# One level of Strassen's algorithm in the first MoE layer of an attention and MoE kernel, with shared tile slots and a new order

## The chip, the core and the metric

The kernel runs on one NeuronCore of a Trainium2 chip. Its time is the device time of one execution in microseconds (us); a figure quoted for a kernel is the median over its runs. One core has a matrix engine (PE, whose weight loads the profile shows apart as PEld), a vector engine (DVE), an activation engine (ACT), a general engine (POOL), and a queue that issues data transfers (SP) to 16 DMA engines. Matmul results land in PSUM, eight banks of 2 KB per partition; everything else lives in SBUF.

## The reference

Local and global attention over 8 batches of 8 heads, then a two-layer MoE block over all 8 x 544 = 4352 rows:

```python
# attention: window of 32 to each side plus 32 global tokens; 512 local tokens, head_dim 64
k_all = concat([k_g, k_l]); v_all = concat([v_g, v_l])
out_g = softmax(scale * q_g @ k_all.T) @ v_all
s_ll = where(abs(i - j) <= 32, scale * q_l @ k_l.T, -1e9)
out_l = softmax(concat([scale * q_l @ k_g.T, s_ll])) @ concat([v_g, v_l])
x = concat([out_g, out_l]).transpose(0, 2, 1, 3).reshape(4352, 512)
# MoE: d_model 512, d_ff 2048
h = x @ w_in
g = where(h >= 1, h, where(h <= -1, 0, (h + 1) ** 2 / 4))
out = g @ w_out
```

## The kernel before

All products run in fp16 on PE. Each operand is held as a high and a low fp16 half (`j` = 0, 1), so one product of two operands is three matmuls: high x high, low x high, high x low.

**Steps.** The program is written as named steps. Those of a batch `b` (0 to 7): loads `Lk`, `Lq`, `Lv`; scales `sk`, `sq`, `sv`; `pk`, `pq`, `pv` split k, q, v into halves and turn them with a DMA transpose; `aa{b}{i}{pr}` (att_a) scores and softmax of two heads for the 128 queries of block i; `ab` (att_b) the product with v; `ax{b}{i}` (att_x) scales the result, splits it (an ACT cast, a DVE or POOL subtraction) and turns it with a DMA transpose of 256 KB; `ga`, `gb` the global queries. The weights come once: `wd`, `ws`, `wh` decode, scale and split w_in (16 blocks `w0` to `w15` of 128 hidden columns, in groups of four), `od`, `oh` do it for w_out.

**MoE.** A *tile* `s` (0 to 15) is 256 local tokens, half a batch (two blocks of att_x). A *group tile* `g0`, `g1` collects the 128 global tokens of four batches. For each pair of hidden blocks moe1 makes `h` in one PSUM bank with 2 x 12 matmuls (4 slices of d_model x 3 halves), 256 token columns wide in a tile and 128 in a group tile; each matmul is preceded by the load of its 128x128 weights. A tile has 8 such pieces, 192 matmuls. Then five instructions make `g`: ACT Relu, two DVE operations, an ACT cast to the high half, a POOL subtraction for the low half (in tiles 0 and 1 sometimes on DVE). moe2 multiplies `g` by w_out: per tile 2 x 48 matmuls 512 columns wide in a second kind of bank, then DVE scales them and a DMA stores them.

**Order.** Nothing in the program runs in the order in which it is written. `segments` cuts the steps into pieces by engine, with the buffers each needs; `schedule` lays them out with a table of costs, taking at every moment the piece with the least due time (`deadlines`) that can start and finds free buffers; `LATER` shifts due times of single steps, in us. What comes out is a fixed order for each of the engines and the SP queue, and each engine works through its own strictly. PSUM has 3 banks for `h` (ps_h, also used by turns and weight splits), 2 for moe2 and norms (ps_o), 2 for scores (ps_s), 1 for att_b (ps_x). SBUF tiles of each kind have slots of their own.

Of the kernel before, what the change touches and what calls it, by code (L numbers as in the profile page):

```python
# [43 lines left out]
class Sketch:  # L44


    def __init__(self):
        self.nc = bacc.Bacc("TRN2", target_bir_lowering=False, num_devices=1)
        self.tiles, self.sizes = {}, {}

    def tile(self, pool, shape, dtype, tag, bufs):
        key = f"{pool.name}.{tag}"
        t = self.nc.dram_tensor(f"sketch{len(self.tiles)}", shape, dtype, kind="Internal").ap()
        self.tiles[t.tensor.name] = (key, bufs, pool.space)
        n = mybir.dt.size(dtype)
        for d in shape[1:]:
            n *= d
        self.sizes[key] = max(self.sizes.get(key, 0), (n + 3) // 4 * 4)
        return t


class Memory:
# [6 lines left out]
    def tile(self, pool, shape, dtype, tag, bufs):  # L69
        key, slot = f"{pool.name}.{tag}", self.taken[f"sketch{self.n}"]  # L70
# [4 lines left out]
        if (key, slot) not in self.slots:  # L75
            nm = f"{pool.name}_{tag}_{slot}"
            self.slots[key, slot] = self.pools[pool.space].tile([128, self.sizes[key] // 4], F32 if pool.space else I32, tag=nm, name=nm)
        n = 1
# [146 lines left out]
def schedule(segs, tiles, hop, slack, landing, ahead):  # L225

    users, queue, slots, many, taken = {}, {}, {}, {}, {}
    for g in segs:
        for nm in g.uses:
            users[nm] = users.get(nm, 0) + 1  # L230
        for nm in g.new:
            tag, n, _ = tiles[nm]
            queue.setdefault(tag, []).append(nm)
            slots[tag] = list(range(n))
            many[tag] = n
        g.left, g.ready = len(g.after), 0.0
    head = {tag: 0 for tag in queue}
    place = {nm: i for q in queue.values() for i, nm in enumerate(q)}
    engines = ("tensor", "vector", "scalar", "gpsimd", "sync")
# [6 lines left out]
    while len(order) < len(segs) or events:  # L246
        went = True
        while went:
            went = False
            for e in engines:  # L250
# [3 lines left out]
                for at, (_, _, g) in enumerate(waiting[e]):  # L254
                    if g.ready > now:
                        continue
                    need = {}
# [15 lines left out]
                for nm in sorted(g.uses - taken.keys(), key=place.get):  # L273
                    tag = tiles[nm][0]
                    taken[nm] = slots[tag].pop(0)
# [18 lines left out]
        if not events:  # L294
            done_ = {g.n for _, g in order}
            g = next((g for g in segs if g.n not in done_), None)
            if g:
                where = [(nm, tiles[nm], place[nm], head[tiles[nm][0]], slots[tiles[nm][0]], [m for m in queue[tiles[nm][0]] if users[m] and place[m] < head[tiles[nm][0]]], queue[tiles[nm][0]][head[tiles[nm][0]]]) for nm in g.new]
# [3 lines left out]
        while events and events[0][0] <= now:  # L302
# [11 lines left out]
            for nm in g.uses:  # L314
                users[nm] -= 1
                if users[nm] == 0:
                    slots[tiles[nm][0]].append(taken[nm])
# [30 lines left out]
def attention_moe(nc, memory, q_l, k_l, v_l, q_g, k_g, v_g, w_in, w_out, out):  # L348
# [19 lines left out]
    class Pool:  # L368
        def __init__(self, name, bufs, space=None):
            self.name, self.bufs, self.space = name, bufs, space  # L370
# [4 lines left out]
    pool = Pool  # L375
# [3 lines left out]
    gp = pool("hidden", 1)  # L379
    stg = pool("stage", 4)  # L380
    tmp = pool("tmp", 4)
    natp = pool("nat", 2)
    ktp = pool("kt", 7)
    kt4p = pool("kt4", 2)
    qtp = pool("qt", 3)
    qgp = pool("qg", 2)
    vp = pool("v", 7)
    v2p = pool("v2", 2)
    sm = pool("small", 2)
    bsm = pool("batch_small", 2)  # L390
    tp = pool("tts", 3)
    pfp = pool("pf", 2)
    ptp = pool("pt", 3)
    pgp = pool("pg", 1)
    xtp = pool("xt", 2)
    xgp = pool("xg", 1)
    xnp = pool("xn", 1)
    rp = pool("moe_t", 2)
    jp = pool("junk", 1)
    ps_h = pool("ps_h", 3, space=PSUM)  # L400
    ps_o = pool("ps_o", 2, space=PSUM)
    ps_s = pool("ps_s", 2, space=PSUM)
    ps_x = pool("ps_x", 1, space=PSUM)
# [59 lines left out]
    def all_sum(o, x, name):  # L463
# [3 lines left out]
        t = ps_s.tile([P, 1], F32, tag="s", name=f"as{name}")  # L467
# [3 lines left out]
    def all_max(o, x, name):  # L471
# [3 lines left out]
        t = ps_s.tile([P, P], F32, tag="s", name=f"am{name}")  # L475
# [19 lines left out]

    W = {}
# [6 lines left out]
    wi = [t.bitcast(F16).rearrange("p (j k c) -> p j k c", j=2, c=P) for t in wi32]  # L503
    wo = [t.bitcast(F16).rearrange("p (j c) -> p j c", j=2) for t in wo32]
# [38 lines left out]
    def w_scale(norms, tag, n, pl):  # L543
# [4 lines left out]
        inverse(t2, s, e, 2.0 ** -51, 2.0 ** -13)  # L548
# [17 lines left out]
    def halves(w, a, s, sid, who):  # L566
# [3 lines left out]
        if who[0] == "e":  # L570
            o = ps_h.tile([P, DM], F32, tag="h", name="wps")
# [22 lines left out]
    def turn(who, o, i):  # L594
# [5 lines left out]
        t = ps_h.tile([P, 8, P], F16, tag="h", name="turn")  # L600
# [765 lines left out]
```

## Time and profile before

| | us |
|---|---|
| runs: median (lowest to highest) of 3 | 972.21 (970.84 to 973.53) |
| profiled execution: first to last instruction | 972.9 |
| PE busy in it | 894.0 |
| DVE busy | 696.5 |
| ACT busy | 582.3 |
| POOL busy | 374.9 |

The profiled execution has no time of its own beside its span; the span stands 0.7 us above the median of the runs, inside their spread. Busy times are unions of the instructions' spans, so two that overlap count once. Matmuls are pipelined: the mean time of one matmul in a group is its way through the array, and what it costs the engine is the distance from one to the next, which the rows that merge a run of matmuls give (their us divided by their count).

### The profile page before, as it was taken

What the parts mean: (1) busy time and instruction counts of PE and PEld (TensorE: products, weight loads), DVE (VectorE), ACT (ScalarE), POOL (GpSimd) and SP (SyncE); (2) the same over time, 40 slices, a digit from 0 to 9 for tenths busy, and PEclk for the clock granted to TensorE, in tenths of its full rate; (3) what the DMA queues carried; (4) which work ended last, traced back from release to release, by engine and by line L of the source; (5) the groups of instructions that cost most, each with busy time, mean ns of one, the idle gap of its engine ahead of it and who ended that gap; (6) DMA issues with size and microseconds to landing.
All of it is one profiled execution on the core that took longest, in us unless ns stands there. A gap on an engine that the chain in (4) does not pass through costs nothing.

```text
span 972.9 us, 24493 instructions
## 1 busy us (share of the span) xinstructions
PE 894.0 (92%) x9375; PEld 633.7 (65%) x9375; DVE 696.5 (72%) x1951; ACT 582.3 (60%) x1405; POOL 374.9 (39%) x390
## 2 busy tenths in 40 slices
PE   0864879987999999999999999999999999999998
PEld 0443657556766776767676777767776777676764
DVE  3889898777876797678754977778767886564432
ACT  4898677666765666567553666567655754344221
POOL 9055655433324333332432424433433343332121
PEclk9877889997999999999999999999999999999999
DMA  9959669699896879789961888678877755244001
GB/s 254 241 138 216 161 135 161 152 161 164 136 187 131 148 135 168 125 139 152 168 128 24 136 148 177 115 131 153 138 153 136 138 113 109 56 86 51 23 2 33
DMA packets 386998, 129.41 MB, mean 133 GB/s; under 512 B 363328, under 2 KB 372544, under 8 KB 386880
## 3 DMA queue, kind: packets, MB, share of 16 engines
q1 hardware_dynamic: 386880, 127.85, 69.1%
q8 instruction: 73, 1.20, 0.5%
q14 instruction: 45, 0.37, 0.1%
HBM read 43.52 MB, written 8.91 MB: 54 GB/s over the span
## 4 chain that ended last, share of the span: by engine, by line
PE 67%; DMA 11%; DVE 8%; ACT 6%; issue 4%; POOL 2%; SPq 1%; ACTq 0%; DVEq 0%; POOLq 0%
PE ps_h_h L1280 30%; PE ps_o_o L1280 28%; PE ps_s_s L1280 5%; PE ps_x_x L1280 4%; DMA pt_pt<-const_pb 3%; DMA stage_st<-in_k_l_dram 2%; DMA qt_qa<-nat_nat 1%; ACT junk_junk L1280 1%; DMA stage_st<-in_moe_w_out_dram 1%; ACT pf_pf L1280 1%; DVE tts_t L1280 1%; DMA stage_st<-in_v_l_dram 1%; POOL const_pb L1280 1%; DVE tmp_tmp L1280 1%; DVE weights_w L1280 1%
## 5 line engine op out<-in xcount | busy, mean ns | idle before, releaser
L1280 PE MATMUL ps_h_h<-xt_xt,weights_w 128*128 128x256 f16 (+1 forms) x3456 | 383.5, 269 | 1.9 <-DVE moe_t_r L1280 1.4
L1280 PE MATMUL ps_o_o<-weights_w,hidden_g 128*128 128x512 f16 x1632 | 374.0, 380 | 3.0 <-DVE tmp_tmp L1280 1.1
L1280 PEld LDWEIGHTS <-weights_w 128*128 128x128 f16 x3456 | 320.8, 99 | 52.3 <-issue 5.0
L1280 POOL TENSOR_TENSOR hidden_g<-moe_t_r,hidden_g 128x512 f16<-128x512 f32 (+1 forms) x142 | 164.4, 1158 | 314.9 <-ACT hidden_g L1280 304.8
L1280 PEld LDWEIGHTS <-hidden_g 128*128 128x128 f16 x1712 | 158.7, 98 | 183.2 <-issue 17.0
L1280 POOL TENSOR_TENSOR const_pb<-pf_pf,const_pb 128x384 f16<-128x384 f32 (+1 forms) x117 | 120.6, 1032 | 225.7 <-DVE const_pb L1280 89.4
L1280 DVE SCALAR_TENSOR_TENSOR ps_h_h<-ps_h_h,batch_small_ms,moe_t_r 128x512 f32<-128x512 f32 (+1 forms) x144 | 104.2, 724 | 105.5 <-ACT moe_t_r L1280 105.3
L1280 ACT ACTIVATE pf_pf<-tts_t,small_nb 128x192 f32<-128x192 f32 (+1 forms) x256 | 117.0, 458 | 97.2 <-DVE small_nb L1280 77.3
L1280 ACT ACTIVATE moe_t_r<-ps_h_h,batch_small_ms 128x512 f32<-128x512 f32 (+1 forms) x144 | 107.8, 749 | 103.9 <-PE ps_h_h L1280 92.4
L1280 ACT CAST hidden_g<-moe_t_r 128x512 f16<-128x512 f32 (+1 forms) x144 | 84.4, 587 | 76.5 <-DVE moe_t_r L1280 76.2
L1280 DVE CUSTOM_DVE_ANT_0 tts_t<-ps_s_s,const_mask,batch_small_q 128x192 f32<-128x192 f32 (+1 forms) x256 | 98.9, 427 | 23.0 <-PE ps_s_s L1280 22.7
L1280 DVE SCALAR_TENSOR_TENSOR moe_t_r<-moe_t_r,batch_small_ms,ps_h_h 128x512 f32<-128x512 f32 (+1 forms) x144 | 102.5, 713 | 2.6
L1280 ACT ACTIVATE junk_junk<-stage_st 128x512 f16<-128x512 f32 (+1 forms) x108 | 67.5, 625 | 45.5 <-DMA stage_st<-in_k_l_dram 14.1
L1280 PE MATMUL ps_x_x<-v_v,pt_pt 128*128 128x64 f16 (+1 forms) x1536 | 68.8, 195 | 10.2 <-DMA pt_pt<-const_pb 7.7
L1280 DVE CAST const_pb<-pf_pf 128x384 f16<-128x384 f32 (+1 forms) x109 | 47.8, 440 | 41.0 <-ACT pf_pf L1280 23.0
L1280 PE MATMUL ps_s_s<-kt_kt,qt_qa 128*128 128x128 f16 (+2 forms) x704 | 69.3, 200 | 8.3 <-DVE small_nb L1280 5.7
L1280 PEld LDWEIGHTS <-pt_pt 128*128 128x128 f16 (+1 forms) x1536 | 61.8, 99 | 22.9 <-DMA pt_pt<-const_pb 10.9
L1280 PEld LDWEIGHTS <-qt_qb 128*128 128x128 f16 x704 | 55.4, 99 | 16.0 <-issue 10.8
L1280 PE MATMUL ps_s_s<-kt_kt,qt_qb 128*128 128x128 f16 (+2 forms) x704 | 65.8, 199 | 0.0
L1280 PEld LDWEIGHTS <-qt_qa 128*128 128x128 f16 x704 | 59.6, 99 | 6.3 <-issue 1.1
L1280 ACT ACTIVATION_READ_ACCUMULATOR pf_pf<-tts_t,small_nb 128x1 f32 x256 | 47.7, 187 | 0.0
L1280 PE MATMUL ps_o_o<-tmp_tmp,const_ones 128*128 128x128 bf16 (+1 forms) x76 | 14.3, 311 | 23.5 <-DVE tmp_tmp L1280 23.4
(170 smaller groups left out, 914.3 us busy)
## 6 DMA issues: line engine op xcount, KB each, us to landing
weights_w<-in_moe_w_in_dram SPq DMA_DIRECT2D x32, 256.0 KB, 4.1
stage_st<-in_q_l_dram SPq DMA_DIRECT2D x32, 256.0 KB, 4.2
qt_qb<-qt_qa SPq DMA_DIRECT2D x64, 128.0 KB, 2.7
stage_st<-in_moe_w_out_dram SPq DMA_DIRECT2D x32, 256.0 KB, 3.7
out_dram<-tmp_tmp SPq DMA_DIRECT2D x30, 256.0 KB, 2.6
stage_st<-in_k_l_dram SPq DMA_DIRECT2D x24, 256.0 KB, 3.8
stage_st<-in_v_l_dram SPq DMA_DIRECT2D x21, 256.0 KB, 4.4
v_v<-v_v SPq DMA_DIRECT2D x16, 128.0 KB, 3.2
```

Of the source, the lines that this page charges most:

```text
L1280: getattr(getattr(tc.nc, engine), op)(*a, **k)
```

## The change

**Strassen.** From tile 3 on (`T["fast"] = 3`), and for both group tiles, the product of w_in and the tokens is cut into 2 x 2 blocks: two groups of four hidden blocks (`f1`, `f2`), two halves of d_model, two halves of the tokens (128 + 128 in a tile, 64 + 64 in a group tile). Seven products P1 to P7 take the place of eight; each is 4 x 6 = 24 matmuls, 128 (or 64) columns wide. A tile has two such rounds (`q` = 0, 1), 2 x 7 x 24 = 336 matmuls. The sums around them: three sums of w_in blocks per round are made once, by matmuls with the identity (`combine`, steps `cb`) into six 4 KB tiles, and one difference overwrites its block of w_in when tile 2 is done with it (`replace`, steps `rp`). The sums of tokens are made per tile in att_x by four POOL subtractions of 256 columns, so that a tile now has four casts, four low halves and four DMA transposes where it had two of each (widths 512, 256, 512, 512 in place of 512, 512). The sums of products are formed in PSUM (P6, P7, P4 add to the bank of P1, P3 to that of P5), with three ACT copies and three DVE additions per round. `g` is made as before, for 4 hidden blocks x 128 tokens at a time, eight times per tile.

**Widths.** Tiles 0 to 2 make `h` for 128 tokens at a time instead of 256: 384 matmuls of 128 columns. The scale of w_in is now common to two groups, so their splits (`wh`) wait for both.

**Rooms.** SBUF tiles of up to 2 KB per partition share 48 slots, all PSUM tiles share the 8 banks, with a cap per kind (`ps_h` 4, `ps_o` 3, `ps_s` 2, `ps_x` 1). `LATER` is a new table that covers the steps of all batches.

```diff
@@ schedule
-                    if need and any(len(slots[tag]) < len(x) + (min(x) > head[tag]) or max(x) - head[tag] >= many[tag] for tag, x in need.items()):
+                    if need and (any(many[tag] - live[tag] < len(x) + (min(x) > head[tag]) or max(x) - head[tag] >= many[tag] for tag, x in need.items())
+                                 or any(len(slots[key]) < len(x) + (min(x) > first[key]) * (ROOMS[key][2] if key in ROOMS else 0) for key, x in rooms.items())):
...
@@ att_x
+        if t == 0 or not FAST(s):
+            XT[s, t] = across(xf, f"x{s}_{t}", who, how)
+            d["xn"] = xf
+            return
+        x1, x2 = d.pop("xn"), xf
+        XT[s, "b"] = across(x2[:, K:], f"xb{s}")
+        for o, y, z in ((x1[:, :K], x2[:, :K], x1[:, :K]), (x2[:, :K], x2[:, K:], x2[:, :K]), (x2[:, K:], x2[:, K:], x1[:, :K]), (x1[:, K:], x1[:, K:], x2[:, K:])):
+            nc.gpsimd.tensor_tensor(out=o, in0=y, in1=z, op=ALU.subtract)
+        XT[s, "c"] = across(x1, f"xc{s}")
+        XT[s, "d"] = across(x2, f"xd{s}")
...
+    def combine(q, a):
...
+        add(ident, f2, 0, True)
+        add(ident, f2, 1)
+        for n, (f, c) in enumerate((((0, 0), (f1, 0), (f1, 1)))):
+            if n:
+                add(negid, f, c)
+            o, sign = CW[q][n][:, a:a + 2], (1.0, 1.0, -1.0)[n]
+            nc.scalar.activation(o[:, :, 0], ps, AF.Copy, scale=sign)
+            nc.vector.scalar_tensor_tensor(o[:, :, 1], ps, sign, o[:, :, 0], op0=ALU.mult, op1=ALU.subtract)
...
+    def moe_f(key, d, x, n, q):
...
+        one = acc("x")
+        prod(one, "P1", True)
+        s = fold(who, "s", n)
+        nc.scalar.copy(s, one)
+        two = acc("z")
+        prod(two, "P5", True)
+        p5 = fold(who, "p", n)
+        nc.scalar.copy(p5, two)
+        prod(one, "P6", False)
+        u2 = fold(who, "u", n)
+        nc.scalar.copy(u2, one)
+        three = acc("y")
+        prod(three, "P2", True)
+        nc.vector.tensor_tensor(out=three, in0=three, in1=s, op=ALU.add)
+        out_of(three, 0, 0)
+        prod(one, "P7", False)
+        nc.vector.tensor_tensor(out=p5, in0=one, in1=p5, op=ALU.add)
+        prod(two, "P3", False)
+        nc.vector.tensor_tensor(out=two, in0=two, in1=u2, op=ALU.add)
+        out_of(two, 0, 1)
+        out_of(p5, 1, 1)
+        prod(one, "P4", False)
+        out_of(one, 1, 0)
...
+CAPS = dict(hidden=8, stage=9, tails=3, tmp=4, ob=3, nat=4, kt=7, qa=3, qb=3, v=7, v2=2, t=5, pt=3, xt=8, xg=1, xn=2, xh=2, r=5, raw=4, sums=6,
+            ps_h=4, ps_o=3, ps_s=2, ps_x=1)
+ROOMS = dict(room=(2048, 48, 4), twin=(4096, 6, 0), bank=(2048, 8, 0))
...
-LATER = {"Lk01": -7.5, "Lk10": 41.8, "Lk11": -14.2, "Lk12": 16.3, "Lk20": 29.4, "Lk21": -32.6, "Lk22": 17.4, "Lo0": 11.5,
+LATER = {"Lk00": -99.8, "Lk01": 23.8, "Lk02": 37.7, "Lk10": 212.4, "Lk11": -53.4, "Lk12": 178.5, "Lk20": 42.4, "Lk21": 24.7,
...
```

PE at the start of tile 9, before (weights `w0` is the first hidden block, `xt` the turned tokens, `ps_h` the bank of `h`):

```order
L1280 MATMUL ps_s_s_0_106<-kt_kt_6_197,qt_qb_2_152 128x64
L1280 LDWEIGHTS weights_w0_0_66
L1280 MATMUL ps_h_h_2_111<-xt_xt_0_139,weights_w0_0_66 128x256
...
L1280 LDWEIGHTS weights_w1_0_67
L1280 MATMUL ps_h_h_2_111<-xt_xt_0_139,weights_w1_0_67 128x256
```

PE in the first round of tile 9, after: the end of P5 (the `twin` tiles are sums of w_in, the first `room` of a moe1 row the tokens), a piece of moe2, then P6 and P3:

```order
L1440 LDWEIGHTS twin_4_168
L1440 MATMUL bank_1_108<-room_44_121,twin_4_168 128x128
L1440 LDWEIGHTS room_45_135
L1440 MATMUL bank_5_145<-weights_w0_0_66,room_45_135 128x512
...
L1440 LDWEIGHTS twin_5_171
L1440 MATMUL bank_2_128<-room_18_133,twin_5_171 128x128
...
L1440 LDWEIGHTS twin_0_155
L1440 MATMUL bank_1_108<-room_29_109,twin_0_155 128x128
```

Each matmul is half as wide and still loads its own weights; between P5 into bank 1 and P3 into the same bank ACT has to copy it, and the order puts 12 matmuls of moe2 and the 24 of P6 there.

PE during the attention of batch 1, before: the end of tile 1's moe1 (`w15`), followed by att_b of block 0:

```order
L1280 LDWEIGHTS weights_w15_0_81
L1280 MATMUL ps_h_h_0_102<-xt_xt_1_142,weights_w15_0_81 128x256
L1280 LDWEIGHTS pt_pt_1_138
L1280 MATMUL ps_x_x_0_160<-v_v_6_206,pt_pt_1_138 128x64
```

The same place after: the scores of block 0, then the first sum of w_in blocks (`cb`, with the identity as weights), then att_b:

```order
L1440 LDWEIGHTS room_24_132
L1440 MATMUL bank_3_105<-room_9_86,room_24_132 128x64
L1440 LDWEIGHTS const_ident_0_85
L1440 MATMUL bank_5_145<-weights_w4_0_70,const_ident_0_85 128x256
...
L1440 MATMUL bank_5_145<-weights_w5_0_71,const_ident_0_85 128x256
L1440 LDWEIGHTS room_8_98
L1440 MATMUL bank_1_108<-room_6_164,room_8_98 128x64
```

Eight of the 64 matmuls of `cb` stand ahead of att_b here; the others follow in pieces of 4 and 8 between the pieces of batch 1's attention, and all of `rp` between the last pieces of tile 2 and the first of tile 3.

DVE in tile 9, before (a piece's first operation writes `ps_h`, its second `moe_t_r`; the cast belongs to attention):

```order
L1280 SCALAR_TENSOR_TENSOR ps_h_h_2_111<-ps_h_h_2_111,batch_small_ms_0_171,moe_t_r_0_173 128x512
L1280 SCALAR_TENSOR_TENSOR moe_t_r_1_172<-moe_t_r_1_172,batch_small_ms_0_171,ps_h_h_1_112 128x512
L1280 TENSOR_SCALAR small_nb_2_143<-small_nb_2_143 128x2
L1280 CAST const_pb0_0_61<-pf_pf_0_131 128x2x224
L1280 SCALAR_TENSOR_TENSOR ps_h_h_0_102<-ps_h_h_0_102,batch_small_ms_0_171,moe_t_r_1_172 128x512
```

DVE in tile 9, after: an addition of a product's bank and a copy stands ahead of an output's two operations, and the low halves of att_x come in between:

```order
L1440 TENSOR_TENSOR bank_3_105<-bank_3_105,room_40_134 128x512
L1440 SCALAR_TENSOR_TENSOR bank_2_128<-bank_2_128,batch_small_ms_0_177,room_28_194 128x512
L1440 SCALAR_TENSOR_TENSOR room_2_88<-room_2_88,batch_small_ms_0_177,room_24_132 128x512
L1440 SCALAR_TENSOR_TENSOR room_28_194<-room_28_194,batch_small_ms_0_177,bank_2_128 128x512
L1440 TENSOR_TENSOR bank_7_131<-bank_7_131,room_1_143 128x512
L1440 SCALAR_TENSOR_TENSOR bank_3_105<-bank_3_105,batch_small_ms_0_177,room_37_150 128x512
```

The two operations per output are the same as before; the additions are new rows in the same queue.

## Rows read from the trace of the kernel before

**Rows 1.** The page: busy time of engines; 40 slices in tenths.
```profile
span 972.9 us, 24493 instructions
PE 894.0 (92%) x9375; PEld 633.7 (65%) x9375; DVE 696.5 (72%) x1951; ACT 582.3 (60%) x1405; POOL 374.9 (39%) x390
PE   0864879987999999999999999999999999999998
PEclk9877889997999999999999999999999999999999
```

**Rows 2.** Stretches: length; busy PE, PEld, DVE, ACT, POOL (count); clock, DMA share, GB/s.
```profile
0.00:300.00 300.00, 229.09 (x2301) 158.68 (x2302) 237.52 (x672) 214.86 (x509) 141.83 (x158) 0.90 0.85 176
300.00:850.00 550.00, 546.81 (x5949) 393.31 (x5948) 405.76 (x1157) 327.34 (x814) 202.86 (x201) 1.00 0.72 131
850.00:973.00 123.00, 118.11 (x1128) 81.71 (x1125) 53.26 (x123) 40.08 (x83) 30.19 (x33) 0.99 0.21 39
```

**Rows 3.** Shorter stretches, the same columns: three of 20 us, one of 50 us.
```profile
200.00:220.00 20.00, 17.27 (x183) 10.88 (x181) 14.81 (x53) 11.74 (x37) 7.24 (x7) 0.92 0.99 154
220.00:240.00 20.00, 14.59 (x247) 12.10 (x246) 16.88 (x63) 12.20 (x38) 5.27 (x8) 0.74 0.99 165
260.00:280.00 20.00, 20.00 (x190) 12.89 (x188) 17.73 (x50) 15.44 (x36) 5.61 (x6) 1.00 0.99 158
...
750.00:800.00 50.00, 50.00 (x596) 36.42 (x594) 41.86 (x128) 30.25 (x75) 19.36 (x19) 1.00 0.70 137
```

**Rows 4.** PE's groups by shape: count, busy us, mean ns, idle before.
```profile
L1280 PE MATMUL ps_h_h<-xt_xt,weights_w 128*128 128x256 f16 x3072 | 360.3, 275 | 1.9 <-DVE moe_t_r L1280 1.4 <-DMA xt_xt<-xn_xh 0.5
L1280 PE MATMUL ps_h_h<-xt_xt,weights_w 128*128 128x128 f16 x384 | 23.2, 219 | 0.0
```

**Rows 5.** The chain that ended last, pieces: start us, us, what.
```profile
303.66 2.62 PE ps_h_h L1280 x24
306.28 0.35 PE ps_x_x L1280 x12
306.63 2.59 PE ps_o_o L1280 x12
```

**Rows 6.** Timeline in group tile g1: start, us, engine, what.
```profile
941.47 4.22 PEld L1280 LDWEIGHTS <-weights_w 128*128 128x128 f16 x72
941.68 4.18 PE L1280 MATMUL ps_h_h<-xt_xt,weights_w 128*128 128x128 f16 x72
...
945.70 2.75 PE L1280 MATMUL ps_o_o<-weights_w,hidden_g 128*128 128x512 f16 x12
```

**Rows 7.** What PE waited for, 300 to 850 us: total, times, longest.
```profile
PE ps_x_x L1280 <- ACT xg_xgf L1280: 1.6, 1, 1.6
PE ps_x_x L1280 <- DMA pt_pt<-const_pb: 1.2, 2, 0.7
```

**Rows 8.** DVE's, ACT's and POOL's groups by shape, as in rows 4.
```profile
L1280 DVE SCALAR_TENSOR_TENSOR ps_h_h<-ps_h_h,batch_small_ms,moe_t_r 128x512 f32<-128x512 f32 x128 | 96.4, 754 | 91.2 <-ACT moe_t_r L1280 91.0
L1280 DVE TENSOR_TENSOR xn_xn<-ps_x_x,small_rc 128x512 f32<-128x512 f32 x32 | 22.0, 686 | 13.5 <-PE ps_x_x L1280 13.5
L1280 DVE TENSOR_TENSOR xn_xh<-xn_xn,xn_xh 128x512 f16<-128x512 f32 x27 | 19.3, 715 | 5.0 <-ACT xn_xh L1280 4.9
L1280 ACT ACTIVATE moe_t_r<-ps_h_h,batch_small_ms 128x512 f32<-128x512 f32 x128 | 98.8, 773 | 88.9 <-PE ps_h_h L1280 80.1 <-POOL hidden_g L1280 6.0 <-PE ps_s_s L1280 2.1
L1280 ACT CAST weights_w<-ps_h_h 128x512 f16<-128x512 f32 x12 | 6.6, 570 | 0.0
L1280 POOL TENSOR_TENSOR hidden_g<-moe_t_r,hidden_g 128x256 f16<-128x256 f32 x16 | 11.7, 728 | 32.4 <-ACT hidden_g L1280 28.6 <-issue 3.3 <-POOL hidden_g L1280 0.5
```

**Rows 9.** DMA transposes of att_x: count, median us from issue to landing.
```profile
xt_xt<-xn_xh SPq DMA_TRANSPOSE x32, 3.3
```

**Rows 10.** Timeline of the end, as in rows 6.
```profile
962.76 5.34 PE L1280 MATMUL ps_o_o<-weights_w,hidden_g 128*128 128x512 f16 x24
...
968.92 1.76 SPq L1280 DMA_DIRECT2D out_dram<-tmp_tmp  x4
```

More of the change, by code (lines that the diff above doesn't have):

```diff
@@ L225, in schedule @@
 def schedule(segs, tiles, hop, slack, landing, ahead):
-    users, queue, slots, many, taken = {}, {}, {}, {}, {}
+    users, queue, slots, many, taken, live, line = {}, {}, {}, {}, {}, {}, {}
     for g in segs:
@@ L273, in schedule @@
                 for nm in sorted(g.uses - taken.keys(), key=place.get):
-                    tag = tiles[nm][0]
-                    taken[nm] = slots[tag].pop(0)
+                    tag, _, _, key = tiles[nm]
+                    taken[nm] = slots[key].pop(0)
+                    live[tag] += 1
+                    while first[key] < len(line[key]) and line[key][first[key]] in taken:
+                        first[key] += 1
                     while head[tag] < len(queue[tag]) and queue[tag][head[tag]] in taken:
@@ L297, in schedule @@
             if g:
[L298 removed]
+                where = [(nm, tiles[nm], place[nm], head[tiles[nm][0]], slots[tiles[nm][3]]) for nm in g.new]
                 raise AssertionError(f"stuck at {g.n} {g.engine} {g.calls[0][0]} {g.uses} needs {[p for p in g.after if p not in done_]} {where}")
@@ L908, in att_a @@
             if "pbx" not in d:
[L909 removed]
+                d["pbx"] = [gp.tile([P, 2, 2, 256], F16, tag="g", name=f"pbx{n}") for n in range(2)]
                 for x in d["pbx"]:
@@ L1041, in attention_moe, with fold, act, middle @@
     GT = {}
-    def moe1(key, d, xt, n, f):
-        h = ps_h.tile([P, 2, n], F32, tag="h", name=f"h{key}_{f}")
-        for u in range(2):
+    def fold(key, nm, n):
+        return rp.tile([P, WG, n], F32, tag="r", name=f"{nm}{key}")
+    def act(key, d, h, n, g, o, low="p"):
+        c = slice(g, g + 1)
+        r = fold(f"{key}_{g}", "r", n)
+        nc.scalar.activation(r, h, AF.Relu, bias=d["hs"][:, c], scale=d["a1"][:, c])
+        nc.vector.scalar_tensor_tensor(h, h, d["a2"][:, c], r, op0=ALU.mult, op1=ALU.max)
+        nc.vector.scalar_tensor_tensor(r, r, d["sg"][:, c], h, op0=ALU.min, op1=ALU.mult)
+        nc.scalar.copy(o[:, :, 0], r)
+        (nc.vector if low == "v" else nc.gpsimd).tensor_tensor(o[:, :, 1], r, o[:, :, 0], op=ALU.subtract)
+    def middle(key, g, t):
+        if (key, g, t) not in GT:
+            GT[key, g, t] = gp.tile([P, WG, 2, P], F16, tag="g", name=f"gt{key}_{g}_{t}")
+        return GT[key, g, t]
+    def moe1(key, d, x, g, t):
+        h = ps_h.tile([P, WG, P], F32, tag="p", name=f"h{key}_{g}_{t}")
+        for u in range(WG):
             m = 0
@@ new lines, in replace @@
+    def replace(q, a):
+        K = DM // 2
+        ps = ps_h.tile([P, 2, 2, P], F32, tag="p", name=f"wr{q}{a}")
+        f1, f2 = 2 * WG * q + a, 2 * WG * q + WG + a
+        n = 0
+        for u in range(2):
+            for i, f in ((ident, f1), (negid, f2)):
+                for j in range(2):
+                    nc.tensor.matmul(ps[:, u], i, w16[f + u][:, j, :K], start=n == 0, stop=True, skip_group_check=True)
+                    n += 1
+        for u in range(2):
+            nc.scalar.copy(wi[f2 + u][:, 0, 0:2], ps[:, u])
+            nc.vector.tensor_tensor(out=wi[f2 + u][:, 1, 0:2], in0=ps[:, u], in1=wi[f2 + u][:, 0, 0:2], op=ALU.subtract)
```

311 lines of the change are left out of this document (185 added, 126 removed), and 150 rows, old and new, of the table LATER.

## The prediction

> **What bounds the kernel now.** The page first [rows 1]: of a span of 972.9 us PE is busy 894.0, and its slices read 9 from the eleventh to the last but one, while of the first ten only two do. Then the stretches [rows 2]: from 300 to 850 us PE is busy 546.81 of 550 at a granted clock of 1.00, with DVE at 405.76 (74%), ACT at 327 and POOL at 203; after 850 us it stays full to the end. Before 300 us it is idle 70.9 us, and the clock averages 0.90. So there are two regimes: a front of 300 us that waits for loads, for the decoding of weights and for the first attention (DVE 237.5 of 300, DMA 0.85), and a stage of 670 us in which PE's own work is the time. In that stage PE's waits, as the trace names them, come to little over 3 us in all, of which two rows stand for the most [rows 7]. What is taken off PE after 300 us should shorten the span by as much, unless something else comes to wait; work added ahead of 300 us may hide in PE's gaps.
>
> **The change, part by part, on PE.** The chain gives what a matmul costs PE [rows 5]: 24 of 256 columns take 2.62 us, 109.2 ns each; 12 of 64 columns 0.35 us, 29.2 ns each; 12 of 512 columns 2.59 us, 216 ns each. At 128 columns the kernel has group tile g1: 72 matmuls, each with its own weight load, stand between 941.68 and 945.70 us, where the next group begins [rows 6]; 4.02 us, 55.8 ns each.
>
> - Fast tiles (3 to 15, thirteen): 192 x 109.2 = 20.97 us become 336 x 55.8 = 18.75 us. Less 2.22 us each, 28.8 us in all.
> - Group tiles: 192 x 55.8 = 10.71 us become 336 x 29.2 = 9.81 us. Less 0.9 us each, 1.8 us.
> - Tiles 0 to 2: 384 x 55.8 = 21.43 us for 20.97, 1.4 us more.
> - `cb`: 64 matmuls of 256 columns, 7.0 us. `rp`: 32 of them, 3.5 us.
>
> That is 30.6 us less and 11.9 us more, net 18.7 us less.
>
> What the additions cost on the path depends on where they stand. The order puts `cb` between the pieces of batch 1's attention. There PE is idle 2.7 and 5.4 us in two stretches of 20 us and the clock falls to 0.74 [rows 3], so at most all 7.0 us hide; but `cb` also brings 12 ACT copies and 12 DVE operations of 512 columns, about 9 us of DVE at 754 ns [rows 8], and DVE is busy 31.7 of those 40 us. I take half, 3.5 us, with 0 and 7 as bounds. `rp` and the narrower tiles meet a PE that is full (20.00 of 20 from 260 to 280 us [rows 3]); I take them whole, 4.9 us.
>
> **On the other engines.** Per fast tile DVE gains six additions of 512 columns from PSUM (686 ns, as the row that scales an attention block [rows 8]), 4.1 us, and one and a half low halves (715 ns), 1.1 us: 5.2 us. ACT gains six copies from PSUM, between 570 and 773 ns each (the cast out of `ps_h` and the Relu [rows 8]), 3.4 to 4.6 us, and 1 us of casts. POOL gains four subtractions of 256 columns at 728 ns, 2.9 us. SP issues two transposes more per tile. A transpose of att_x lands 3.3 us after its issue [rows 9], which bounds the DMA time of one and a half more by 5 us per tile; the lower bound is what 384 KB take at the 131 GB/s that the stage moves at a DMA share of 0.72, 3 us at most [rows 2].
>
> Does any of them become the bound? moe1 of the stage from 300 to 850 us covers some 10.5 tiles and a group tile. DVE would come to 405.8 + 10.5 x 5.2 = 460 of about 526 us, 88%; ACT to 73%, POOL to 44%, DMA to between 0.81 and 0.85. DVE's 88% is high, but busy here counts the way of an instruction through the pipeline, and from 750 to 800 us DVE is at 41.86 of 50 with PE at 50.00 [rows 3]. What counts is then the meeting points inside a round: P6 needs the bank of P1 copied, P7 that of P6, P3 that of P5, P4 the addition after P7. The order puts 24 or more other matmuls between each pair, 1.34 us at least, while a copy takes 0.6 to 0.8 us plus ACT's queue. I put 3 us for added waits in the stage; the lower bound is 0, the upper one is the rival below.
>
> **The front's order.** All loads, decodes and the attention of batches 0 and 1 are laid out anew, with freer slots. Up to tile 3 each engine does the same work as before plus `cb` and `rp`. The front's idle 70.9 us are what a better order could draw on and a worse one could add to; nothing in the trace prices an order. I take 3 us less, with 12 less and 10 more as bounds, about a sixth of the idle time.
>
> **Sum.** 972.9 - 30.6 + 3.5 + 4.9 + 3 - 3 = 950.7 us. The profiled span is 0.7 us above the runs' median, so 950 us. The end is no term: after the last matmuls (962.76 + 5.34 us) come one DVE scaling and a store [rows 10], and both stay.
>
> **A rule against this.** The row shows 55.8 ns for a matmul of 128 columns with its weight load, sustained over 72 of them, and the loads take 4.22 us for the 72 beside them [rows 6]. The Trainium skill, page "TensorE: Matmul & The Clock Gate", section "Back-to-back issue gap", gives for streams of weight loads and matmuls a sustained 81 ns at 128 columns and 131 ns at 512. By it 336 matmuls would take 27.2 us, 6.2 us more than a tile's moe1 takes now, and thirteen tiles would lose 81 us: the change would be a large loss. The trace does not agree at either width (55.8 ns at 128 and 216 ns at 512 [rows 5]), so the sum goes by the rows, and the rule stands below as a rival.
>
> **The rivals.**
>
> *The front gains more than 3 us.* The order covers all steps and `cb` fills gaps in which the clock had dropped. For it: the 70.9 idle us. Against it: DVE at 79% over the whole front [rows 2], and no less work for it. With 12 us from the front and `cb` hidden, 972.2 - 30.6 + 4.9 - 12 = 934.5; chance 0.12 of a time below 942.
>
> *Waits in the fast tiles take half of the gain.* DVE at 88% runs late in stretches with attention, and PE meets it four times a round. At 0.11 us for each of the 120 meeting points (13 tiles and 2 group tiles, 2 rounds, 4 each) 13 us are lost: 963. For it: DVE's share. Against: 84% without a wait now. Chance 0.16 of 960 to 969.
>
> *Slower: the bank that is copied too late.* In a fast round PE can't go on in the bank of P1 until ACT, strict in its order, has copied it. If ACT or DVE stands behind attention work at these points (one operation of 512 columns ahead in a queue is 0.6 to 0.8 us [rows 8]), each of the 120 points may cost 0.4 us, 48 us in all: 972.2 - 22 + 48 = 998. It decides from 0.2 us a point (22 us / 120). For it: three of eight banks are held through a round, where a piece now holds one. Against: the trace shows PE waiting for a freed `h` bank almost never (idle 1.9 us before 3072 matmuls [rows 4]). Chance 0.07, at 975 to 1000.
>
> *The weight load sets the pace at 128 columns.* If long runs of such matmuls went at what the loads of moe1 take when they don't overlap, the fast tiles would lose; already at 62.4 ns a matmul (20.97 us / 336) a fast tile takes as long as now. Group tile g1's 55.8 ns, and the 0.0 us of idle time ahead of its 384 [rows 4], speak against it. At 70 ns, 13 x 336 x 14.2 ns = 62 us more than summed: 1012. Chance 0.01. (The skill's rule above would give this case.)
>
> *The change does not pay.* The front loses 10 us, `cb` lies on the path whole and the stage waits 8 us: 950 + 13 + 3.5 + 5 = 971. Chance 0.05.
>
> **How the numbers follow.** The forecast, 942 to 960, has 0.59; with 0.12 below and 0.16 between 960 and 969. A change of 0.3% (2.9 us) is about what this measurement can tell from none, so all of these count as faster: 0.87. The 0.05 of no gain is within 0.3% for the most part, 0.04, and 0.01 goes to slower, with the 0.07 and 0.01 of the two rivals: 0.09. For the range I leave out 0.05 below 936 and about 0.14 above 967.
>
> **What would show it.** In the profile of the changed kernel, 24 matmuls of 128 columns in a tile's moe1 take 1.34 us; if 1.5 or more, the load paces them. PE's busy time falls by 15 to 20 us and its idle time in the first 300 us stays within 10 us of 71. From 300 to 850 us PE reads at least 99% busy; 97% would mean the second rival, and PE rows of a fast tile that wait for ACT or DVE the third. DVE rises to 85 to 90% in that stage. The prediction is wrong if the stage after 300 us is not 25 to 29 us shorter for the same work, or if the front moves by more than 12 us.

## The result and the profile after

The changed kernel takes 946.16 us (median of 4 runs, 945.80 to 948.33), the kernel before 971.6 beside it: a ratio of 0.9732, with a 95% interval from 0.9711 to 0.9752. The prediction of 950 us, within 936 to 967, holds. That is in part luck: what Strassen's level saves was put too high and the gain of the front too low, as the experiments show.

The page of the changed kernel, the lines that answer to [rows 1]:

```profile
span 944.0 us, 30674 instructions
PE 861.5 (91%) x12204; PEld 642.3 (68%) x12207; DVE 786.0 (83%) x2079; ACT 642.9 (68%) x1545; POOL 434.0 (46%) x450
PE   0466889998989998999999999999999999999998
PEclk9979999999999999999999999999999999999999
```

The span is 28.9 us shorter; PE's busy time falls by 32.5 us and its idle time rises by 3.6. By the ratio of the runs the gain is 26.0 us: the two profiled executions stand further apart than the medians. Every run that lists both has a time 1.7 to 2.1 us above its span (945.80 and 944.0 us here), so the 972.9 us of before belong to a time near 975 us, above all its runs and not close to their median; the 945.80 us are the shortest of the changed kernel's runs. The work that was counted off PE is only 18.7 us. The clock line tells where most of the rest is from: before, six of the first ten slices stand below 9, now one. Its three stretches, against [rows 2] with the same columns:

```profile
0.00:300.00 300.00, 229.64 (x3123) 173.72 (x3126) 248.62 (x694) 225.79 (x543) 144.33 (x159) 0.98 0.86 180
300.00:850.00 550.00, 541.59 (x7951) 407.04 (x7949) 484.56 (x1294) 379.83 (x937) 258.73 (x258) 1.00 0.80 141
850.00:944.00 94.00, 90.27 (x1138) 61.54 (x1135) 52.81 (x93) 37.33 (x68) 30.89 (x34) 1.00 0.17 37
```

In the first 300 us PE is busy as long as before (229.64 for 229.09) and so idle as long, 70.4 us, but at a clock of 0.98 instead of 0.90. From 300 to 850 us DVE is at 88%, as summed, and PE at 98.5%. Two of the shorter stretches of [rows 3], and one with the most work on DVE:

```profile
220.00:240.00 20.00, 18.20 (x359) 16.24 (x357) 18.89 (x60) 15.16 (x40) 9.54 (x12) 1.00 0.82 112
260.00:280.00 20.00, 16.77 (x187) 10.72 (x185) 15.79 (x44) 12.98 (x33) 7.12 (x8) 1.00 0.78 168
...
600.00:700.00 100.00, 99.67 (x1444) 75.05 (x1443) 95.83 (x263) 75.30 (x192) 48.31 (x45) 1.00 0.94 160
```

Where the clock stood at 0.74, from 220 to 240 us, it is 1.00; where PE was full, from 260 to 280 us, it now has gaps; and DVE reaches 96% from 600 to 700 us while PE is busy 99.67 of the 100. The seven products of a round cost what [rows 6] said. The timeline of PE inside a fast tile (start, us, what) has three of them in a row, 1.34 us from one start to the next, 55.8 ns a matmul (the 1.50 us of a line count the last matmul's way through the array as well):

```profile
610.34 1.50 PE L1440 MATMUL bank<-room,twin 128*128 128x128 f16 x24
611.68 1.50 PE L1440 MATMUL bank<-room,weights_w 128*128 128x128 f16 x24
613.02 1.50 PE L1440 MATMUL bank<-room,twin 128*128 128x128 f16 x24
```

PE's waits from 300 us on (total, times, longest), against [rows 7]:

```profile
PE bank L1440 <- DMA room<-const_pb: 4.3, 3, 2.1
PE bank L1440 <- ACT room L1440: 2.1, 1, 2.1
PE bank L1440 <- DMA room<-room: 1.1, 1, 1.1
PE bank L1440 <- DVE room L1440: 0.8, 2, 0.4
```

That is 8 us where there were 3. More than half is waiting for the turned probabilities of an attention block (`const_pb`, turned by a DMA transpose), in three places; the copies and additions inside the fast rounds, 120 meeting points, show at most three waits (the rows for ACT and DVE). The new instructions beside PE, against [rows 8]:

```profile
L1440 DVE TENSOR_TENSOR bank<-bank,room 128x512 f32<-128x512 f32 x52 | 35.6, 692 | 18.0 <-PE bank L1440 17.8 <-ACT room L1440 0.2
L1440 DVE SCALAR_TENSOR_TENSOR room<-room,batch_small_ms,bank 128x512 f32<-128x512 f32 x102 | 75.0, 739 | 0.5
L1440 DVE SCALAR_TENSOR_TENSOR room<-room,batch_small_ms,room 128x512 f32<-128x512 f32 x52 | 49.2, 947 | 0.6 <-ACT room L1440 0.2
L1440 ACT COPY room<-bank 128x512 f32<-128x512 f32 x78 | 44.2, 579 | 17.1 <-PE bank L1440 15.8 <-POOL small_amv L1440 0.5 <-ACT room L1440 0.5
L1440 POOL TENSOR_TENSOR room<-room,room 128x256 f32<-128x256 f32 x39 | 32.3, 827 | 5.6 <-DVE room L1440 2.8 <-DVE batch_small_ms L1440 0.5 <-DVE small_nb L1440 0.5
```

The addition and the copy cost what was taken for them, POOL's subtraction 827 ns where 728 were taken. DVE's operations that make `g` look dearer where the sum lies in SBUF, as it does for one output in four: 947 ns for 739. The mean misleads here. The same operations with shortest, median and longest time (both widths):

```profile
L1440 DVE SCALAR_TENSOR_TENSOR room<-room,batch_small_ms,bank x114: 461/739/749, 110.6 to 926.0; 128x512 f32<-128x512 f32 x102, 128x256 f32<-128x256 f32 x12
L1440 DVE SCALAR_TENSOR_TENSOR room<-room,batch_small_ms,room x60: 466/747/1740, 299.6 to 922.4; 128x512 f32<-128x512 f32 x52, 128x256 f32<-128x256 f32 x8
```

Of the 52 wide ones 36 take 744 ns on average. The other 16 take 905 to 1740 ns, and each of them ends between 542 and 551 ns after a POOL operation beside it has ended. One of them, and the POOL operation:

```profile
805.71 1.74 DVE L1440 SCALAR_TENSOR_TENSOR room<-room,batch_small_ms,room 128x512 f32<-128x512 f32 x1
805.74 1.16 POOL L1440 TENSOR_TENSOR room<-room,room 128x512 f16<-128x512 f32 x1 [2.03 <-ACT room L1440]
```

So what costs DVE time is not the place of the sum as such: these operations, with both tensors in SBUF, are held up by POOL in 16 of 52 cases. The operations that read one tensor from a bank and write to SBUF, 102 as wide, stay at 749 ns or less, and of those that read and write a bank one in 102 goes beyond 759.

### The profile page after: what moved, and what is told of

Its sections match the earlier page's. It is cut to its first block, busy times and chain, and to the rows that moved or that the text cites. A ratio compares the mean times of both kernels' runs of the same rounds, so it can differ in the third digit from the quotient of the medians.

```text
span 944.0 us, 30674 instructions
## 1 busy us (share of the span) xinstructions
PE 861.5 (91%) x12204; PEld 642.3 (68%) x12207; DVE 786.0 (83%) x2079; ACT 642.9 (68%) x1545; POOL 434.0 (46%) x450
## 4 chain that ended last, share of the span: by engine, by line
PE 63%; DVE 9%; DMA 7%; ACT 3%; issue 2%; SPq 2%; POOL 1%; DVEq 0%; ACTq 0%; POOLq 0%
PE bank L1440 63%; DVE room L1440 5%; DMA room<-const_pb 3%; ACT room L1440 2%; DMA room<-room 2%; DVE bank L1440 1%; DMA room<-in_k_g_dram 1%; DMA room<-in_k_l_dram 1%; SPq L1440 1%; DMA room<-in_q_l_dram 1%; ACT junk_junk L1440 1%; DVE const_pb L1440 1%; SPq L1442 1%; POOL const_pb L1440 1%; POOL room L1440 1%
## 5 line engine op out<-in xcount | busy, mean ns | idle before, releaser
L1440 PEld LDWEIGHTS <-room 128*128 128x128 f16 (+2 forms) x5136 | 288.2, 98 | 223.5 <-issue 25.0
L1440 PE MATMUL bank<-weights_w,room 128*128 128x512 f16 x1632 | 373.1, 380 | 3.6 <-ACT room L1440 2.1
L1440 POOL TENSOR_TENSOR room<-room,room 128x512 f16<-128x512 f32 (+5 forms) x200 | 223.7, 1125 | 212.3 <-ACT room L1440 185.0
L1440 PE MATMUL bank<-room,weights_w 128*128 128x128 f16 (+1 forms) x4032 | 235.2, 216 | 6.7 <-DVE room L1440 4.0
L1440 POOL TENSOR_TENSOR const_pb<-room,const_pb 128x384 f16<-128x384 f32 (+1 forms) x117 | 124.2, 1063 | 225.5 <-DVE const_pb L1440 81.4
L1440 ACT CAST room<-room 128x512 f16<-128x512 f32 (+3 forms) x212 | 122.0, 583 | 81.3 <-DVE room L1440 65.3
L1440 ACT ACTIVATE room<-room,small_nb 128x192 f32<-128x192 f32 (+1 forms) x256 | 117.2, 459 | 55.2 <-DVE small_nb L1440 45.0
L1440 PE MATMUL bank<-room,room 96*128 96x64 f16 (+3 forms) x2816 | 128.3, 196 | 9.4 <-DMA room<-const_pb 6.1
L1440 PE MATMUL bank<-room,twin 128*128 128x128 f16 (+1 forms) x2160 | 123.1, 216 | 3.3 <-DMA room<-room 2.4
L1440 PEld LDWEIGHTS <-twin 128*128 128x128 f16 x2160 | 115.5, 98 | 6.3 <-DMA room<-room 2.5
L1440 DVE CAST const_pb<-room 128x384 f16<-128x384 f32 (+1 forms) x109 | 51.4, 474 | 19.9 <-DMA room<-const_pb 13.2
```

The costliest lines, as they stand in the source:

```text
L1440: getattr(getattr(tc.nc, engine), op)(*a, **k)
```

## The experiments

**How they were made.** The order comes from a planner, so a small edit of the program moves everything. In all but f1, f2 and f3 the plan is made from the unedited program and the edit is applied when the instructions are issued: each engine keeps the order of the kernel named. Differences are taken between ratios to the kernel before (x 971.6 us); the intervals are some 0.25% to either side, so less than about 3 us is not told from none.

**The theory** was that PE's own work is the time of the fast tiles, and that the front gains because PE meets fewer idle stretches that bring its clock down. **The rivals**: waits at the meeting points eat a good part of the gain; DVE, at 88%, is as much the bound as PE.

**One product more, one less.**

```diff
-                for engine, op, a, k in again[n]:
+                for engine, op, a, k in again[n] * (2 if marks[0] == "P2" else 1):      # e1
+                for engine, op, a, k in again[n] if marks[0] != "P4" else []:           # e2
```

> The changed kernel in the same order on every engine, with the product P2 of every fast round issued twice, the second pass over the first: 26 x 24 matmuls of 128 columns and 4 x 24 of 64 columns more on PE, nothing more elsewhere. That is the count of eight products of which Strassen's level leaves seven. If PE's own work is the time in the fast tiles, the kernel takes 624 x 55.8 ns + 96 x 29.2 ns = 34.8 + 2.8 = 37.6 us more, 983.8 us. If waits at the meeting points of a round (a bank not yet copied, an addition not yet made) hold part of the time, the added matmuls fall into them and cost less: with half of the gain lost to waits, as the second rival had it, about 25 us, 971.

> The changed kernel in the same order, with the product P4 of every fast round left out (so the output lacks it): 26 x 24 matmuls of 128 columns and 4 x 24 of 64 fewer on PE, all else as it is. If PE's work alone is the time, 37.6 us less, 908.6 us. DVE, at 88% of the stage from 300 to 850 us, would stand at 93% of a stage that is 28 us shorter: if DVE or its queue then sets the pace in the stretches with attention, the gain is under 30 us, 916 us or more, and PE shows waits for DVE's tiles that it does not show now.

e1: 978.01 us, ratio 1.0069 (1.0043 to 1.0094), 32.7 us more than the changed kernel for 37.6 us of PE. e2: 931.77 us, 0.9592 (0.9566 to 0.9619), only 13.6 us less for the same amount. From 300 to 850 us, e1 and then e2:

```profile
300.00:850.00 550.00, 543.91 (x8026) 413.87 (x8024) 465.71 (x1231) 365.24 (x891) 248.25 (x246) 1.00 0.76 137
```

```profile
300.00:850.00 550.00, 524.74 (x7472) 381.68 (x7470) 487.87 (x1307) 380.65 (x943) 260.42 (x260) 0.99 0.82 143
```

So PE's work is the time for seven products and for eight, and the step from eight to seven is worth 87% of its matmuls (78 to 95% within the intervals). e1 also prices the rest of the change: with eight products it is 6.7 us slower than the kernel before (1.0069), while the narrower matmuls cost some 8.4 us (an estimate: 13 x 0.46 and 2 x 0.5 us for the tiles of the fast rounds, 1.4 for tiles 0 to 2) and `cb` and `rp` are 10.5 us of work. Of these 18.9 us the new order and its higher clock win back some 12, so they pay for the additions and not for more; what makes the kernel faster is the product left out. PE's work is hardly the time for six products: PE then waits 25 of 550 us. For what, the waits of e2 from 300 us on tell:

```profile
PE bank L1441 <- DMA room<-const_pb: 13.2, 10, 3.0
PE bank L1441 <- ACT room L1441: 4.8, 5, 1.4
PE bank L1441 <- POOL room L1441: 2.6, 5, 0.7
...
PE bank L1441 <- DVE room L1441: 0.7, 2, 0.4
```

The turned probabilities again, ten times and 13.2 us of the 25. What binds next is attention in the main. The rows for ACT, POOL and DVE, 8.1 us, are in part the fast tiles' own: all five waits for POOL stand ahead of moe2, which needs the low halves of `g`. By these three runs the changed kernel stands close to the point where PE's work and these chains take equally long.

**Combine and replace at a quarter.**

```diff
+   ... w16[f + u][:, j, c * K:(c + 1) * K], ..., drop=(not first))      # e3, combine
+   ... w16[f + u][:, j, :K], ..., drop=i is negid or j == 1)            # e4, replace
+                for engine, op, a, k in [c for c in again[n] if not c[3].pop("drop", False)]:
```

> The changed kernel in the same order, with 48 of the 64 identity matmuls of the combine steps left out (the sums of weights are then incomplete); their ACT and DVE instructions stay. 48 x 109.2 ns = 5.2 us. Wholly on the path: 5.2 us less, 941.0 us. Half hidden in PE's gaps, as summed: 2.6 us less, 943.6. Wholly hidden: no change. If these matmuls are what keeps the granted clock up between 200 and 240 us, the time rises instead, by up to some 5 us.

> The changed kernel in the same order, with 24 of the 32 identity matmuls of the replace steps left out (the differences of weights are then incomplete). 24 x 109.2 ns = 2.6 us. As summed (PE full there): 2.6 us less, 943.6 us. If they stand in gaps of PE: no change.

e3: 945.93 us, ratio 0.9737 (0.9712 to 0.9762). e4: 945.66 us, 0.9734 (0.9707 to 0.9762). Neither differs from the changed kernel's 0.9732 (in e4 at most 2.6 us were expected, less than these intervals can tell). For `cb` the trace shows why. PE around its gap (length; busy, count; clock, DMA share, GB/s), in the changed kernel:

```profile
212.00:216.00 4.00, 3.58 (x70) 1.00 0.82 123
216.00:220.00 4.00, 2.98 (x82) 1.00 0.86 164
```

and in e3, with two rows of its timeline (the bracket is the idle time ahead):

```profile
212.00:216.00 4.00, 0.43 (x12) 0.72 0.75 107
216.00:220.00 4.00, 3.99 (x73) 0.50 0.78 147
```

```profile
216.01 0.82 PE L1440 MATMUL bank<-room,room 128*128 128x64 f16 x12 [3.58 <-DMA room<-const_pb]
...
217.79 4.18 PE L1440 MATMUL bank<-room,weights_w 128*128 128x128 f16 x48
```

Without the combine matmuls PE waits 3.58 us for a turned block that comes at the same time as ever (the twelve matmuls stand at 215.85 us in the changed kernel), the clock then falls to its lower level (1.2 of 2.4 GHz), and 48 matmuls of 128 columns take 4.18 us, which take 2.84 there. The work filled a gap, and the filled gap kept the clock. The replace matmuls do stand where PE is full, from 255 to 261 us, but not long before its gaps (16.77 of 20 us from 260 to 280). The 12 matmuls of moe2 behind the first of these gaps, and the last piece of the replace steps, in the changed kernel and then in e4:

```profile
272.97 2.75 PE L1440 MATMUL bank<-weights_w,room 128*128 128x512 f16 x12
...
282.80 0.38 PE L1440 MATMUL bank<-weights_w,const_ident 128*128 128x256 f16 x2
```

```profile
272.30 0.69 PE L1440 MATMUL bank<-room,room 128*128 128x128 f16 x7 [2.65 <-DMA room<-room]
272.81 3.92 PE L1440 MATMUL bank<-weights_w,room 128*128 128x512 f16 x12
...
283.04 0.38 PE L1440 MATMUL bank<-weights_w,const_ident 128*128 128x256 f16 x2
```

What e4 saves by 261 us is gone by 283: the tile that PE waits for comes only 0.4 us earlier, so PE waits 2.65 us where it waited 1.63, and the same 12 matmuls then take 3.92 us for 2.75, at a clock of 0.60 from 272 to 276 us where it was 1.00.

**The front of the kernel before, filled by hand.**

```diff
+                    times = 4 if st[:2] == "wd" else 3 if st[:4] in ("ab00", "ab01", "ab02") and st[4] != "3" else 2 if st[:4] in ("ab10", "ab11", "ab12") else 1
-                for engine, op, a, k in again[n]:
+                for engine, op, a, k in again[n] * times:
```

> The kernel before in its own order, with matmuls of its front issued again over the same bank: the four of each decode step wd four times, the twelve of the steps ab00 to ab02 three times (but for the last pair of heads) and of ab10 to ab12 twice. That is 192 matmuls of 128 columns and 360 of 64, 10.7 + 10.5 = 21.2 us of PE at full clock, and nothing else. If the low granted clock of the front is what the idle stretches of PE bring, and costs the kernel before some 14 us that the changed kernel does not pay, the mean clock of the first 300 us rises from 0.90 to 0.95 or more, and the time stays or falls by up to 10 us in spite of 21 us more work. If the clock does not answer, or the front is not paced by PE, the clock stays near 0.90, and the time stays or rises by up to 10 us.

978.3 us, ratio 1.0045 (1.0029 to 1.0061): 4.4 us slower for 21.2 us more work. Its first 300 us:

```profile
0.00:300.00 300.00, 242.76 (x2805) 178.91 (x2808) 237.19 (x663) 211.93 (x498) 138.48 (x155) 0.93 0.85 173
```

PE is busy 13.7 us longer, not 21.2, and the clock rises from 0.90 to 0.93, less than the 0.95 expected. By hundreds of us it answers where batch 1's attention stands (0.93 to 0.98 from 200 to 300 us), but little in the first hundred (0.83 to 0.87). So the clock does answer to filled gaps, and four fifths of the filler cost no time; but the filler put in blindly does not bring the clock that the changed kernel has, and the time rises.

**Other plans.** Strassen off everywhere (f1), the old `LATER` (f2), Strassen from tile 2 on (f3); here the order is laid out anew.

```diff
-T = dict(late=1, fast=3, cb=200, ...
+T = dict(late=1, fast=99, cb=200, ...      # f1, with group tiles by moe1
+LATER = (that of the kernel before)        # f2
+T = dict(late=1, fast=2, cb=200, ...       # f3
```

> The changed kernel without Strassen in any tile: tiles and group tiles by 128 columns at a time, 384 (192 of 64... here 128 columns in a group tile) matmuls each, no combine or replace steps; rooms, caps and the table LATER as in the changed kernel, laid out anew for the changed steps. PE has 13 x 48 x 55.8 ns = 34.8 us and 2 x 0.9 = 1.8 us more than the changed kernel, and 10.5 us less for combine and replace. If the front's gain is that of rooms and order alone, the front keeps its clock (0.95 or more in the first 300 us) and the kernel takes 972.9 + 7.4 (narrower tiles) - 14 = 966 to 971 us; if the combine steps carry it, the clock falls back to 0.92 or less and the time is 975 to 985, slower than before.

> The changed kernel with the table LATER of the kernel before in place of its own; Strassen, rooms, caps and widths as changed. If the new table made the front's gain, the front falls back by about its 14 us of clock and more idle time, and the order of the fast tiles is that of due times alone: 958 to 975 us. If rooms and Strassen's steps carry it, the time stays within 4 us of the changed kernel's, 942 to 950.

> The changed kernel with Strassen from tile 2 on (one tile more: 336 matmuls of 128 columns for 384, 2.7 us less on PE; the replace steps come a tile earlier). If PE's work in the front were the time, 943.5 us. Since 5.2 us less of combine work and 2.6 us less of replace work brought nothing, no change or a loss is expected: 945 to 955 us, since the table was searched for tile 3.

f1: 1027.93 us, 1.0558 (1.0533 to 1.0584). f2: 978.65 us, 1.0050 (1.0027 to 1.0073). f3: 1029.17 us, 1.0574 (1.0547 to 1.0600). All three times lie outside what was expected. f3 differs from the changed kernel by one tile, less work, and an order that its table was not made for; that costs 82 us. The first 300 us of f1, the first two stretches of f2, and then of f3:

```profile
0.00:300.00 300.00, 230.23 (x3058) 175.69 (x3063) 235.69 (x620) 207.00 (x476) 141.52 (x155) 0.94 0.76 164
```

```profile
0.00:300.00 300.00, 231.96 (x2954) 169.76 (x2957) 246.45 (x648) 215.26 (x508) 140.99 (x156) 0.91 0.79 168
300.00:850.00 550.00, 530.34 (x7653) 398.11 (x7650) 480.80 (x1276) 371.08 (x922) 248.51 (x248) 0.99 0.80 142
```

```profile
0.00:300.00 300.00, 226.01 (x2908) 167.48 (x2912) 253.04 (x690) 225.72 (x542) 145.34 (x161) 0.95 0.84 179
300.00:850.00 550.00, 509.08 (x7220) 383.80 (x7218) 448.18 (x1184) 350.35 (x855) 231.01 (x235) 0.97 0.75 133
```

f3 leaves PE idle 41 us in the stage that was full, f2 20 us. And f2 has back the front of before: a clock of 0.91. So rooms and `cb` alone do not raise the front's clock, and Strassen under the old table gains nothing. f1, with the new table and no `cb` at all, has 0.94 there, between the 0.91 of f2 and the 0.98 of the changed kernel. Both point to the new table as the larger part and `cb` as the smaller one. It is not shown: all three runs are new plans, a plan alone can cost 82 us, and the new table under the kernel before was not tried. f1 can't price Strassen, since it is disturbed in the same way.

**DVE's load.** The 52 low halves of att_x on POOL (h1), one more DVE instruction behind each (h2), h1 with P4 left out (h3), and the casts of the probabilities of batches 2 to 7 on ACT (h4):

```diff
+                    engine = "gpsimd" if k.pop("low", False) else engine                # h1, h3
+                            tc.nc.vector.scalar_tensor_tensor(k["out"], k["out"], 1.0, k["out"], op0=ALU.mult, op1=ALU.max)   # h2
+                    if k.pop("cast", False):                                            # h4
+                        engine, op = "scalar", "copy"
```

> The changed kernel in the same order, with the four low-half subtractions that att_x makes per fast tile (39 of 512 columns at 768 ns, 13 of 256 at 697 ns, 39 us in all) issued on POOL in place of DVE, at 1275 and 707 ns there, 59 us. PE's work stays. If DVE, at 88% from 300 to 850 us, is what makes the attention blocks late for which PE waits after 300 us (8 us in all), up to 5 us less: 941 to 946. If POOL's own part of the attention chain (the low halves of the probabilities, 1.06 us each) is then late, up to 5 us more.

> The changed kernel in the same order, with one DVE instruction more behind each of those 52 subtractions (the maximum of the low half with itself), some 0.7 us each, 36 us more on DVE; nothing else changes. If DVE has no slack left in the stretches with attention, the time rises by 8 us or more, to 954 or above, with PE waiting for the turned probabilities; if it has, by under 3 us.

> The kernel without the product P4 (931.8 us, 14.4 less than the changed kernel for 37.6 us less work on PE), in the same order, with the 52 low-half subtractions on POOL as well (the output lacks P4). If DVE's share is what ate the rest of that gain, 39 us less of DVE return much of it: 925 us or less. If the chain of one attention block (its latency through DVE, ACT, POOL and a DMA transpose) and not DVE's load sets the pace, no change within 3 us, or a loss, as POOL is a link of that chain.

> The changed kernel in the same order, with the cast of the probabilities to their high half (const_pb) on ACT in place of DVE in batches 2 to 7: 96 casts, 45 us off DVE (449 and 500 ns each), 51 us on ACT (557 and 501 ns each, as its 15 casts of the front). The cast then follows the exponential on the same engine, and POOL stays as it is. If DVE's load is what makes the attention late (36 to 45 us more of it cost some 13 us), 5 to 10 us less: 936 to 941, which beats both kernels. If the chain is late through ACT as well, or ACT's queue, strict in its order, holds the copies of the fast rounds back behind these casts, no change or up to 10 us more.

h1: 954.67 us, ratio 0.9781 (0.9754 to 0.9809), 4.8 us slower than the changed kernel. h2: 960.96 us, 0.9864 (0.9834 to 0.9894), 12.8 us slower. h3: 936.6 us, 0.9609 (0.9581 to 0.9637), no different from e2. h4: 947.57 us, 0.9746 (0.9719 to 0.9772), no different from the changed kernel. The added instructions of h2, 45.5 us in its trace (their mean of 881 ns is lengthened by a few of up to 1533 ns, the median is 693), and one wait of PE from 300 us on:

```profile
L1444 DVE SCALAR_TENSOR_TENSOR room<-room 128x512 f16<-128x512 f16 x39 | 34.3, 881 | 1.3
L1444 DVE SCALAR_TENSOR_TENSOR room<-room 128x256 f16<-128x256 f16 x13 | 11.2, 863 | 0.4
```

```profile
PE bank L1442 <- DMA room<-const_pb: 8.9, 5, 2.9
```

and h4 from 300 to 850 us:

```profile
300.00:850.00 550.00, 540.82 (x7872) 403.38 (x7869) 443.99 (x1196) 411.95 (x1016) 250.90 (x256) 0.99 0.77 141
```

More work on DVE costs 0.28 us for each us of the added instructions, and PE's wait for the attention blocks doubles (8.9 us for 4.3). Less work on it brought nothing: over the whole kernel DVE is busy 40 us less in h4 (88% to 81% from 300 to 850 us) and ACT 38 us more; in h3, beside e2, DVE is busy 17 us less, where 39 were expected, and POOL 50 us more. No run relieves DVE without loading another link of the attention chain (DVE, ACT, POOL and the DMA transpose, in strict queues), so a gain may have been eaten there. Nor does every added load cost: h1 (POOL) and h2 (DVE) are slower, h3 (POOL) and h4 (ACT) are not. What is shown is that PE waits for the end of that chain, the turned `const_pb`: 4.3 us in the changed kernel, 8.9 in h2, 13.2 in e2. Whether DVE's load, the length of the chain, or DVE and POOL holding each other up (as in the 16 long operations above) makes it late stays open. Neither a shorter chain nor a third `const_pb` buffer, which would let blocks overlap more, was tried. No version here that computes the whole output beats the changed kernel.

## Why the prediction was right, point by point

**PE bounds the stage, and matmuls taken off it shorten the span.** Right for this change, by e1 and the 1.34 us per product. Its size was a little high: a product's matmuls pay 87%, so the 30.6 us, which count from eight products of 256 columns, are more like 26: 32.7 less the 7.0 us by which 13 tiles and two group tiles cost more in matmuls of half the width (13 x 0.46 and 2 x 0.5). This is an estimate, since no run has 256 columns in this order.

**`cb` 3.5 us, `rp` and narrower tiles 4.9.** As a price of what could be saved, too dear: three quarters of `cb` and of `rp` were worth nothing within some 3 us each (for `rp`, whose three quarters are 2.6 us of work, the waits and the clock in e4's trace say more than the time). That PE was full from 260 to 280 us before was no ground to charge `rp` whole, since what follows it now waits anyway.

**The front's order, -3 us.** This is the step that failed. PE's idle time there is what it was (70.4 for 70.9 us), within the mark set for it, but its busy time holds the added combine and replace work at no extra length. Over the whole span PE's busy time fell by 13.8 us more than the counted work (32.5 - 18.7). Half-clock time accounts for that: at 0.90, 229.09 us of busy time hold some 23 us that full clock would save, at 0.98, 229.64 hold some 5 (estimates from [rows 2] and the stretches above). Their difference is 18; the 4 us by which it exceeds the 13.8 are busy time that no row here explains, and some 3 us of the whole belong to the choice of the two executions (28.9 us between them, 26.0 by the runs). The prediction named the clock of 0.74 beside `cb` and priced only idle time. It expected PE's busy time to fall by 15 to 20 us; 32.5 is outside, and mainly for this cause. The clock alone also passes the 12 us beyond which the prediction called itself wrong for the front, although the time lies in its range; the other half of that mark, 25 to 29 us for the same work behind 300 us, can't be read off, since the new order moves work across that line.

**Added waits, 3 us.** Measured 5 (8.3 for 3.2). Right in size, wrong in place: more at the attention blocks than in the fast tiles. The mark of 99% for PE from 300 to 850 us came out at 98.5%.

**The sum.** On PE's own account 972.9 - 30.6 (Strassen) + 11.9 (all that is added) - 13.8 (the rest of the fall, the clock in the main) + 3.6 (idle time) = 944.0, the span; it closes because the 13.8 are what was left over. Against the prediction's 950.7 that is 6.7 us less: the clock gives 10.8 us more than the front was credited with, and the half of `cb` that was taken as hidden, 3.5, is work all the same (the idle time, 3.6 for 3, hardly differs). The time came out within 4 us of 950 because the front's gain, far above its 3 us, met matmuls that pay less than their full price. What single terms would give back if undone is another question, and the runs answer it: eight products instead of seven 32.7, three quarters of `cb` and of `rp` nothing.

**The rivals.** *The front gains more*: its mechanism came about (the clock, `cb` in the gaps), though not its time below 942. *Waits in the fast tiles* and *the bank copied too late*: at most three waits at 120 points, 3 us, against the 13 and 48 us of these rivals. *The weight load sets the pace*: it did not, with 55.8 ns in the fast tiles; the sustained 81 ns of the Trainium skill, page "TensorE: Matmul & The Clock Gate", section "Back-to-back issue gap", does not hold in this trace. *The change does not pay*: this had 0.05. f2 comes out on that side (978.65 us), but under a table made for another program, so it does not tell what the front of before would have cost the changed kernel; the profile of before could not tell how good the new table is.

## What to carry to other kernels

Where one engine is full, price a cut by what runs beside it: here eight to seven products paid 87%, seven to six 36%. A run with one unit more and one with one unit less shows on which side of the knee a kernel stands. Matmuls placed where PE would idle can be free twice, as in e3: they take no time of their own and keep the clock for what follows. Before reading a mean as the price of an operation, look at its median and its longest case. In a kernel whose order is planned, test an edit in the frozen order and never by a new plan, since a plan made for another program (82 us here) hides any edit.

## What the runs showed of the hardware

A DVE scalar_tensor_tensor of 128x512 fp32 with both tensors in SBUF takes 744 ns on average in 36 of 52 cases and 905 to 1740 ns in the other 16, each of which ends 542 to 551 ns after a POOL operation beside it; with one tensor in PSUM and the output in SBUF none of 102 takes more than 749 ns. In this kernel a sum that is read again is held up less in its bank. During one wait of PE of 3.58 us the clock fell to 0.50 and stayed there for the 4 us of full work behind it, in which 48 matmuls took 47% longer than in the kernel that had filled the gap. Behind a wait of 2.65 us (e4) the clock was 0.60 over 4 us, and 12 matmuls of 512 columns took 3.92 us for 2.75.
